# Unread full-array products in front of the scores, and a second weight pair fetched ahead, in a fused attention and gated-MLP kernel

## The chip, the cores and the metric

The kernel runs on one core of one Trainium2 chip. The core has a matrix engine (TensorE, here PE, with PEld for the loads of its stationary operand), a vector engine (VectorE, DVE), a scalar engine for activations (ScalarE, ACT), a general engine (GpSimd, POOL) and a queue from which most transfers are issued (SyncE, SP). The time is device microseconds for one execution; the number that counts is the median of several runs. One further execution was profiled.

## The reference

One transformer block with 2048 rows of 640 features, 32 heads of 20 features each, and a gated MLP of width 1728. Only these lines matter:

```
h  = x + attention(layernorm(x), wqkv, wo)      # softmax(q k^T / sqrt(20)) v, 32 heads
h2 = h + ((ln(h) @ w_gate) * (ln(h) @ w_up)) @ w_down
```

Inputs and weights are bf16; the output is h2.

## The kernel before

**Score steps.** The 32 heads are eight groups of four. A head takes 32 partitions of a 128-partition tile, so the scores of four heads are four products that each use 32 rows of the array (L497). Their keys are a 128-column slice of `kT` and their queries 512 (or 256) columns of `qa` or `qb`. Products are collected until a score tile `sc` of 1536 columns, three PSUM banks, is full. There are two such tiles, and one step of the main loop fills one. In all there are 683 steps. ACT then takes the exponential of the tile into `E` (L510). In some steps the last 512 columns go to DVE instead, which computes the exponential by a polynomial in four instructions (L538, L547, L548, L543); ACT then handles 1024 columns. The values product takes `E` as its moving operand and `vx` as its stationary one, with 32 output columns for each head (L690), and collects in `acc`.

**Order.** The Python code is a planner. It runs through the steps one by one and writes down every engine's instructions in a fixed order; nothing is reordered on the chip. It keeps its own clocks in `at`: `at["pe"]` for PE, `at["dve"]` for DVE, `at["exp"]` for the end of the last exponential, and `at["slot"]` for the times at which the score tiles come free. In each step it calls `emit_S` (scores and exponential), `emit_AV` (values products), events that are due, and then `run_job`, which fills PE up to a moment a little ahead of ACT's next need. After that `spare` gives DVE what is left of its time. `x_takes` decides whether DVE takes a third of a tile; one of its conditions is that DVE's clock is not far ahead of PE's.

**Jobs.** The rest of the block is cut into generators. `job_proj` and `job_V` make q, k and v (L292, L306). `job_out` multiplies by `wo` (L926), adds x, and makes the second layer norm and its transposes (L272). `job_glu` computes gate and up products (L999 when 512 rows are handled at once, L1017 in `glu_pair` for 256), and `job_y` multiplies by `w_down` (L1058) and stores. Each `yield` tells the planner how long the piece takes on PE. Most of these products use all 128 rows and 128 columns of the array; transposes and products with the identity do too.

**Keep-warm products.** After step 58, where no job ran and there is room by the planner's clocks, `keep_warm` issues two products of the identity with 512 columns of `kT[0]` into a `mi` bank that nothing reads (L467). There are 69 such pairs.

**Weights of the gated MLP.** `w_up` and `w_gate` come in seven pairs of tiles, `fp` 0 to 6, each tile 320 KB (L972, issued from SP). They sit in a pool with two buffers for each name, `wu` and `wg`, so two pairs fit at a time. `job_glu` is run for the first query block whole, then for halves of 256 rows: its keys are (0,0), (1,0), (2,0), (2,2), (3,0). It asks for a pair when the pair before it starts. When it starts its last pair it fetches pair 0 for the next job (`late["next"]`). In the later jobs pairs 3 to 6 are resident, in the tiles of the queries that are no longer needed (`load_res`, once the last query block begins), and only pairs 0 to 2 are streamed. After the last score step `last_tail` finishes the last half block.

Of the kernel before, what the change touches and what calls it, by code (L numbers as in the profile page):

```python
# [36 lines left out]
BANK = 512  # L37
# [17 lines left out]
WARM, LEAD = 58, 3  # L55
# [4 lines left out]
RES_STEPS = 3  # L60
WO_NS, SUMS_NS, ROOT_NS, ROWS_NS = 1500, 6000, 5000, 5000
END_OF_TIME = 10 ** 9
X_LEAST, X_OUT, X_SOON = 3, 6, 4
E_BUFS = 6
SHIFT = 544.0
# [13 lines left out]
def kernel(  # L79
# [11 lines left out]
    nc = tc.nc  # L91
# [22 lines left out]
    ident = const.tile([P, P], BF16, name="ident")  # L114
# [15 lines left out]
    kT = [qkp.tile([P, S], BF16, name=f"kT{g}") for g in range(NG)]  # L130
# [12 lines left out]
    at = {"pe": 0, "dve": 0, "mi": 0, "acc": 0, "slot": [0, 0], "exp": 0, "av": {}}  # L143
# [140 lines left out]
    def q_of(g, b, c0, w):  # L284
        return qb[g][:, c0:c0 + w] if b == NB - 1 else qa[g][:, b * QB + c0:b * QB + c0 + w]
# [47 lines left out]
    for s, (p, g, lo, hi, _) in enumerate(segs):  # L333
        w = PASS[p][2]
# [28 lines left out]
    cur = {"key": None, "gen": None, "fresh": True}  # L363
# [23 lines left out]
    def first():  # L387
        return urgent and (opens.get(urgent[0][0], 0) < at["pe"] + SWITCH or not (waiting or jobs or cur["gen"]))

    def step():  # L390
        if cur["fresh"] and (first() or waiting):
            if cur["gen"] is not None:
                jobs.appendleft((cur["key"], cur["gen"]))
            cur["key"], cur["gen"] = (urgent if first() else waiting).popleft()
        c = advance()
        if c == WAIT:
            waiting.append((cur["key"], cur["gen"]))
            cur["gen"] = None
            c = advance() if jobs and not any(w[0][1:] == jobs[0][0][1:] for w in waiting) else NEXT
        if c is None:  # L400
            return None
        if c == FREE:
            advance()
            return FREE
        if cur["fresh"] and c not in (END, NEXT):
            at["pe"] = max(at["pe"], at["mi"] if cur["key"] != ON_ACC else 0) + SWITCH
        cur["fresh"] = c in (END, NEXT)
        if cur["fresh"]:
            if cur["key"] != ON_ACC:
                at["mi"] = max(at["mi"], at["dve"] + LAT)  # L410
        else:
            at["pe"] += c
        return c

    def advance():
        if cur["gen"] is None:
            if not jobs:
                return None
            cur["key"], cur["gen"] = jobs.popleft()
        try:  # L420
            return next(cur["gen"])
        except StopIteration:
            done.add(cur["key"])
            cur["gen"] = None
            return END

    def ensure(key):
        while key not in done:
            if step() is None:
                raise RuntimeError(f"no job for {key}")  # L430
# [30 lines left out]

    COST = {"T": 300, "v": 680, "nf": 780}

    def keep_warm():
        ps = bank()
        for _ in range(2):
            nc.tensor.matmul(ps[:], lhsT=ident[:], rhs=kT[0][:, 0:BANK], start=True, stop=True)  # L467
# [19 lines left out]
    def emit_S(i):  # L487
        sc = scp.tile([P, EW], F32, name="sc")
        us, n = tiles[i]
        for s, kt, j, _ in us:  # L490
            p, g = segs[s][0:2]
            ensure(("k", g, kt // TPB))
            ensure(("q", PASS[p][0], g))
        for s, kt, j, o in us:
            p, g = segs[s][0:2]
            b, c0, w = PASS[p]
            nc.tensor.matmul(  # L497
                sc[:, o:o + w],
                lhsT=kT[g][SLOT * j:SLOT * (j + 1), kt * P:(kt + 1) * P],
                rhs=q_of(g, b, c0, w)[SLOT * j:SLOT * (j + 1), :],  # L500
                start=True, stop=True)
        begin = max(at["pe"], at["slot"][-2])
        at["pe"] = begin + S_NS
        start = max(at["exp"], begin + S_EXP)
        n_act, took = n, None
        if start == at["exp"] and x_takes(i):
            n_act = n - BANK
            took = emit_x(sc[:, n_act:n], [(s, kt, j, o - n_act) for s, kt, j, o in us if o >= n_act])
        e = ep.tile([P, EW], BF16, name="E")
        exps = nc.scalar.activation(e[:, 0:n_act], sc[:, 0:n_act], ACT.Exp, bias=EXP_BIAS, scale=SM_SCALE)  # L510
        if took is not None:
            tc.declare_no_dep(exps.ins, took.ins, reason="both only read the score tile, in different banks")
        run = EXP_NS + n_act * EXP_COL
        free = start + run + EXP_END
        at["slot"].append(free if took is None else max(free, at["dve"] + LAT))
        at["exp"] = start + run
        for s, kt, j, o in us:
            if o < n_act:
                av_q.append((i, s, kt, j, e[:, o:o + PASS[segs[s][0]][2]]))
# [4 lines left out]
    def x_takes(i):  # L524
        us, n = tiles[i]
        s = us[-1][0]
        return (n == EW and segs[s][4] == "only" and (PASS[segs[s][0]][0] < LAST_B or X_LAST(segs[s][0])) and last_tile[s] - i >= X_LEAST and len({u[0] for u in us}) == 1
                and len(x_open) < 2 and at["dve"] < at["pe"] + TOL and len(x_live) < X_OUT)

    def emit_x(ps, us):  # L530
        s = us[0][0]
        w = PASS[segs[s][0]][2]
        v = xp.tile([P, BANK], F32, name="xv", bufs=2)
        u = v[:].bitcast(U16).rearrange("p (n h) -> p n h", h=2)[:, :, 0]
        t = xp.tile([P, BANK], F32, name="xt", bufs=2)
        e = xp.tile([P, BANK], I16, name="xe", bufs=X_OUT)
        dve(690)
        took = nc.vector.tensor_scalar(v[:], ps, X_SCALE, X_BASE, ALU.mult, ALU.max)  # L538
        x_live.append((s, us[-1][1], us[-1][2]))
        x_left[s] = x_left.get(s, 0) + 1  # L540

        def last():
            nc.vector.scalar_tensor_tensor(e[:], t[:], X_R, v[:], ALU.mult, ALU.add)  # L543
            x_left[s] -= 1
            x_put.append([(now["i"], s, kt, j, e[:, o:o + w].bitcast(BF16)) for s, kt, j, o in us])
        x_open.append((s, deque([
            lambda: nc.vector.scalar_tensor_tensor(t[:], u, X_P, u, ALU.add, ALU.mult),  # L547
            lambda: nc.vector.scalar_tensor_tensor(t[:], t[:], X_Q, u, ALU.add, ALU.mult),  # L548
            last])))
        x_last[0] = x_open[-1]  # L550
        return took
# [233 lines left out]
    def gen_ln(ch):  # L785
        ts = range(ch * TPB, (ch + 1) * TPB)
        mv = small.tile([P, TPB, 2], F32, name="mv")
        while at["pe"] < x_at.get(ch, END_OF_TIME) and not now["forced"]:
            yield WAIT
# [96 lines left out]
        nc.sync.dma_start(qsp[g][:, QA:S], qb[g][:])  # L886


    late = {"res": {}}

    def open_late():
        rx.release()
# [80 lines left out]
        return view  # L973

    def load_w(fp, st):
        if fp == 0 and "next" in late:
            st["w", fp] = late.pop("next")
        elif fp in st["res"]:
            st["w", fp] = st["res"][fp]
        else:  # L980
            st["w", fp] = [w_tile(src, fp, late["w"].tile([P, KT * FPW], BF16, name=nm))
                           for nm, src in (("wu", B_w_up), ("wg", B_w_gate))]
# [28 lines left out]
    def glu_pair(st, fp, f2, c0, n):  # L1011
# [13 lines left out]
                yield 216 * n // QB  # L1025
        yield NEXT

    def job_glu(st, ts, order=tuple(range(FP)), more=False):
        c0, n = ts[0] * P, len(ts) * P
        hold = {}  # L1030
        if "hh" not in st:
            st["hh"] = [late["h"].tile([P, QB], BF16, name=f"hh{f}") for f in range(2 * FP)]
        for k, fp in enumerate(order):
            for nx in order[k:k + 2]:
                if ("w", nx) not in st:
                    load_w(nx, st)
            if more and k == FP - 1:
                ahead = {"res": {}}
                load_w(0, ahead)
                late["next"] = ahead["w", 0]  # L1040
            for f2 in range(2):
                if n <= HW and end["pool"] is None:
                    yield from glu_pair(st, fp, f2, c0, n)
                    continue
                for m in range(2):
                    yield from glu_sum(st, fp, f2, m, c0, n, hold)
        for fp in range(FP):
            del st["w", fp]

    def job_y(st, ts, store_halves=False):  # L1050
        for t in ts:
# [184 lines left out]
    i = 0  # L1236
# [134 lines left out]
```

## Time and profile before

| what | value |
|---|---|
| median of 3 runs | 942.64 us (939.83 to 942.7) |
| the profiled execution | 945.22 us, of which the span is 943.4 us |
| mean granted PE clock over the span | 0.984 |
| first to last exponential of a score tile | 15.4 to 899.3 us |
| PE, waiting for a score tile to be freed by ACT | 43.6 us in 103 waits |

How the rows of the profile are read: a group has the line, the engine, the operation, output<-inputs by name, the shapes, the count, then the busy time and the mean duration in ns, then the idle time of the engine directly before these instructions and what ended it. In a row of windows the columns are the stretch, its length, the busy time and number of instructions of PE, PEld, DVE, ACT and POOL, the clock that PE was granted (1.00 is full), the share of the DMA engines and GB/s. In a row of the timeline the first two numbers are start and duration in us, and the bracket gives the idle time before it and its releaser. Matmuls are pipelined, so that the durations of neighbours overlap, and exponentials overlap their neighbours by some 0.1 to 0.4 us.

### The profile page before, as it was taken

Reading aid. Unit: us, or ns where it says so; the run is one execution under the profiler, and the core shown is the slowest. Engines: PE = TensorE matmul, PEld = TensorE weight load, DVE = VectorE, ACT = ScalarE, POOL = GpSimd, SP = SyncE. Lnnn points to the kernel's source line nnn. Section 1 sums busy time; section 2 is a strip of 40 time slices with the busy share of each in tenths; the row PEclk is TensorE's granted clock in tenths of the full one; section 3 lists DMA queues with packets and bytes.
Section 4 is the critical chain, followed back from the end, with each engine's and each line's share of the span. In section 5 each row is a group of like instructions: output and inputs, shape, how many; then the busy total and the mean of one; then the engine's idle time right before and its main releaser. Section 6 shows DMA issues by size and latency. Waiting matters only on the chain.

```text
span 943.4 us, 20070 instructions
## 1 busy us (share of the span) xinstructions
PE 832.4 (88%) x8087; PEld 348.2 (37%) x8087; DVE 668.8 (71%) x1333; ACT 882.6 (94%) x719; POOL 62.2 (7%) x160
## 2 busy tenths in 40 slices
PE   8788898889988899988898998998898889978897
PEld 5233232222232222332233333444433444434565
DVE  7673358898888888888887667777688667372342
ACT  6999999999999999999999999999899999998941
POOL 4210011000000000000000000000000000000000
PEclk9999999999999999999999999899899999998999
DMA  6000010011150122115100322011601301002310
GB/s 189 28 2 1 1 31 21 13 35 27 41 163 13 29 69 61 48 55 198 27 13 21 85 69 63 3 42 53 179 6 41 87 10 48 15 8 69 77 43 17
DMA packets 75515, 47.20 MB, mean 50 GB/s; under 512 B 20412, under 2 KB 71752, under 8 KB 75416
## 3 DMA queue, kind: packets, MB, share of 16 engines
q1 hardware_dynamic: 75416, 45.86, 17.8%
q8 instruction: 65, 1.06, 0.5%
q14 instruction: 34, 0.28, 0.1%
HBM read 38.53 MB, written 7.30 MB: 49 GB/s over the span
## 4 chain that ended last, share of the span: by engine, by line
ACT 44%; PE 31%; issue 15%; DVE 8%; DMA 1%; SPq 0%; ACTq 0%
ACT E L510 44%; PE sc L497 7%; PE acc L690 5%; PE mi L1058 4%; PE mi L999 3%; PE mi L1017 3%; PE mi L292 2%; PE f L999 2%; PE f L1058 2%; PE mi L306 1%; DMA wg<-in_B_w_gate_dram 1%; DVE xt L548 1%; PE mi L926 1%; DVE st L194 1%; PE mi L467 1%
## 5 line engine op out<-in xcount | busy, mean ns | idle before, releaser
L510 ACT ACTIVATE E<-sc 128x1536 bf16<-128x1536 f32 (+1 forms) x683 | 865.1, 1434 | 19.5 <-PE sc L497 16.1
L497 PE MATMUL sc<-qa,kT 32*128 32x512 bf16 (+1 forms) x1920 | 203.3, 341 | 41.7 <-ACT E L510 32.8
L497 PEld LDWEIGHTS <-kT 32*128 32x128 bf16 x2816 | 85.9, 92 | 261.2 <-issue 215.2
L690 PE MATMUL acc<-E,vx 128*32 128x256 bf16 (+1 forms) x2624 | 172.8, 329 | 0.6 <-ACT E L510 0.6
L538 DVE TENSOR_SCALAR xv<-sc 128x512 f32<-128x512 f32 x144 | 98.8, 688 | 47.1 <-PE sc L497 45.3
L548 DVE SCALAR_TENSOR_TENSOR xt<-xt,xv 128x512 f32<-128x512 f32 x144 | 102.5, 719 | 0.8
L543 DVE SCALAR_TENSOR_TENSOR xe<-xt,xv 128x512 int16<-128x512 f32 x144 | 102.2, 714 | 0.9
L547 DVE SCALAR_TENSOR_TENSOR xt<-xv 128x512 f32<-128x512 uint16 x144 | 101.3, 717 | 0.3
L292 PE MATMUL mi<-lnT,wp 128*128 128x512 bf16 x305 | 83.8, 381 | 8.9 <-DVE kT L299 3.8
L613 POOL TENSOR_TENSOR on<-asb,bc 128x256 bf16<-128x256 f32 (+1 forms) x35 | 37.1, 1059 | 698.3 <-DMA bc<-scr 433.8
L690 PEld LDWEIGHTS <-vx 128*32 128x32 bf16 x2816 | 56.5, 96 | 67.3 <-issue 66.6
L497 PE MATMUL sc<-qb,kT 32*128 32x256 bf16 (+1 forms) x896 | 69.7, 293 | 11.6 <-ACT E L510 10.8
L1058 PE MATMUL mi<-wd,hh 128*128 128x320 bf16 x350 | 63.3, 302 | 2.2 <-DVE xr L1062 2.2
L1058 PEld LDWEIGHTS <-hh 128*128 128x128 bf16 x448 | 38.0, 97 | 39.6 <-issue 28.5
L1022 DVE CAST u<-mi 128x256 bf16<-128x256 f32 (+1 forms) x42 | 17.7, 422 | 40.3 <-PE mi L1017 39.9
L292 PEld LDWEIGHTS <-wp 128*128 128x128 bf16 x310 | 25.1, 97 | 53.0 <-issue 39.1
L690 PE MATMUL acc<-xe,vx 128*32 128x512 bf16 (+1 forms) x192 | 44.5, 330 | 0.0
L467 PE MATMUL mi<-kT,ident 128*128 128x512 bf16 x138 | 41.7, 384 | 2.1 <-DVE hh L1024 0.6
L926 PE MATMUL mi<-wo,on 128*128 128x320 bf16 x224 | 40.9, 309 | 2.2 <-DVE xr L930 2.1
L999 PE MATMUL mi<-ln2T,wu 128*128 128x512 bf16 (+1 forms) x140 | 39.1, 389 | 3.9 <-DVE hh L1007 3.9
L999 PE MATMUL mi<-ln2T,wg 128*128 128x512 bf16 (+1 forms) x140 | 38.7, 382 | 3.4 <-DVE u L259 3.4
L299 DVE TENSOR_SCALAR kT<-mi,one_row 128x512 bf16<-128x512 f32 x30 | 22.4, 745 | 26.8 <-PE mi L292 26.5
(150 smaller groups left out, 630.3 us busy)
## 6 DMA issues: line engine op xcount, KB each, us to landing
wu<-in_B_w_up_dram SPq DMA_DIRECT2D x24, 320.0 KB
wg<-in_B_w_gate_dram SPq DMA_DIRECT2D x24, 320.0 KB
bc<-scr SPq DMA_DIRECT2D x80, 64.0 KB
qsp<-qa SPq DMA_DIRECT2D x8, 384.0 KB
xr<-in_A_x_dram SPq DMA_DIRECT2D x16, 160.0 KB
bc<-scr SPq DMA_DIRECT2D x76, 32.0 KB
out_dram<-xr SPq DMA_DIRECT2D x14, 160.0 KB
wd<-in_B_w_down_dram SPq DMA_DIRECT2D x13, 160.0 KB
```

The source lines that it names most:

```text
L292: nc.tensor.matmul(ps[:], lhsT=wslice(m, g, c), rhs=lnT[:, c, ch * QB:(ch + 1) * QB], start=(c == 0), stop=(c == KT - 1))
L467: nc.tensor.matmul(ps[:], lhsT=ident[:], rhs=kT[0][:, 0:BANK], start=True, stop=True)
L497: nc.tensor.matmul(sc[:, o:o + w], lhsT=kT[g][SLOT * j:SLOT * (j + 1), kt * P:(kt + 1) * P], rhs=q_of(g, b, c0, w)[SLOT * j:SLOT * (j + 1) ...
L510: exps = nc.scalar.activation(e[:, 0:n_act], sc[:, 0:n_act], ACT.Exp, bias=EXP_BIAS, scale=SM_SCALE)
L538: took = nc.vector.tensor_scalar(v[:], ps, X_SCALE, X_BASE, ALU.mult, ALU.max)
L543: nc.vector.scalar_tensor_tensor(e[:], t[:], X_R, v[:], ALU.mult, ALU.add)
L547: lambda: nc.vector.scalar_tensor_tensor(t[:], u, X_P, u, ALU.add, ALU.mult),
L548: lambda: nc.vector.scalar_tensor_tensor(t[:], t[:], X_Q, u, ALU.add, ALU.mult),
L690: nc.tensor.matmul(acc["t"][SLOT * j:SLOT * (j + 1), 0:w], lhsT=vx[kt][:, VS * h:VS * h + SLOT], rhs=e, start=(acc["n"][j] == 0), stop=(ac ...
L926: nc.tensor.matmul(ps[:, 0:HALF], lhsT=on[g][:, t * P:(t + 1) * P], rhs=wo[g][:, cs], start=(g == 0), stop=(g == NG - 1))
L999: nc.tensor.matmul(ps[0:M, 0:n], lhsT=st["w", fp][k][:, c, f2 * P:f2 * P + M], rhs=st["ln2T"][:, c, c0:c0 + n], start=(c == 0), stop=(c == ...
L1058: nc.tensor.matmul(ps[:, 0:HALF], lhsT=st["hh"][f][0:K, t * P:(t + 1) * P], rhs=late["Wd"][f][0:K, cs], start=(f == 0), stop=(f == 2 * FP ...
```

## The change

There are two edits. The planner now keeps a list, `full`, of what it has put on PE with the full array: every piece of a job (apart from the short piece of a normalisation job) and the keep-warm pairs. `cool()` asks whether less than 520 ns of it lies in the last 2400 ns by the planner's clock. If so, `emit_S` issues one product of the identity with 512 columns of `kT[0]` into the first bank of the score tile, just before the scores that overwrite it, and adds 216 ns to PE's clock. Nothing reads that product. The second edit fetches pair 1 of the next GLU job, as well as pair 0: it is asked for when a GLU job has ended.

```diff
+FULL_IN, FULL_NS = 2400, 520
...
         else:
             at["pe"] += c
+            if cur["key"][0] != "nf" or c > 780 or c == 515:
+                full.append((at["pe"], c))
         return c
...
+    full = deque()
+
+    def cool():
+        now_ = max(at["pe"], at["slot"][-2])
+        while full and full[0][0] < now_ - FULL_IN:
+            full.popleft()
+        return sum(f[1] for f in full) < FULL_NS
+
     def keep_warm():
+        full.append((at["pe"], 430))
         ps = bank()
...
             ensure(("q", PASS[p][0], g))
+        if i > WARM and cool():
+            at["pe"] = max(at["pe"], at["slot"][-2]) + 216
+            full.append((at["pe"], 216))
+            nc.tensor.matmul(sc[:, 0:BANK], lhsT=ident[:], rhs=kT[0][:, 0:BANK], start=True, stop=True)
         for s, kt, j, o in us:
...
-        if fp == 0 and "next" in late:
-            st["w", fp] = late.pop("next")
+        if fp in late["next"]:
+            st["w", fp] = late["next"].pop(fp)
...
+    def load_next(fp):
+        ahead = {"res": {}}
+        load_w(fp, ahead)
+        late["next"][fp] = ahead["w", fp]
+
     def job_glu(st, ts, order=tuple(range(FP)), more=False):
...
             if more and k == FP - 1:
-                ahead = {"res": {}}
-                load_w(0, ahead)
-                late["next"] = ahead["w", 0]
+                load_next(0)
...
         for fp in range(FP):
             del st["w", fp]
+        if more:
+            load_next(1)
```

More of the change, by code (lines that the diff above doesn't have):

```diff
@@ L886, in spill @@
         nc.sync.dma_start(qsp[g][:, QA:S], qb[g][:])
-    late = {"res": {}}
+    late = {"res": {}, "next": {}}
     def open_late():
```

## The prediction

> **What bounds the kernel now.** I read the page first, then ACT's waits from 60 us on, then windows of 3.41 us around each fall of the PE clock, then ACT's exponentials place by place.
>
> ```profile
> span 943.4 us, 20070 instructions
> ...
> PE 832.4 (88%) x8087; PEld 348.2 (37%) x8087; DVE 668.8 (71%) x1333; ACT 882.6 (94%) x719; POOL 62.2 (7%) x160
> ```
>
> ```profile
> ACT E L510 <- PE sc L497: 14.1, 20, 3.2
> ```
>
> ACT is busy for 94% of the span and its exponentials (E from sc, L510) set the pace of the loop. What can be won inside the loop is the time in which ACT waits for scores: 14.1 us after the first 60 us, in 20 waits. The next table shows where the clock is (columns: stretch, its length, busy time and instructions of PE, PEld, DVE, ACT, POOL, then the granted clock, DMA share, GB/s).
>
> ```profile
> 308.92:312.33 3.41, 3.41 (x19) 0.65 (x16) 2.83 (x5) 2.64 (x3) 0.00 (x0) 0.50 0.02 5
> 585.39:588.81 3.42, 2.77 (x45) 1.42 (x40) 3.19 (x9) 3.25 (x4) 1.02 (x1) 1.00 0.06 19
> 588.81:595.63 6.82, 5.92 (x57) 2.69 (x57) 4.78 (x9) 5.59 (x5) 0.00 (x0) 0.50 0.01 2
> ...
> 660.49:663.90 3.41, 3.38 (x22) 1.08 (x21) 0.84 (x3) 1.33 (x2) 0.00 (x0) 0.50 0.23 40
> ...
> 677.55:680.97 3.42, 3.42 (x17) 1.19 (x20) 2.94 (x5) 2.45 (x3) 0.00 (x0) 0.50 1.08 318
> ...
> 715.10:718.52 3.42, 3.42 (x21) 1.11 (x19) 3.18 (x4) 2.48 (x3) 1.43 (x1) 0.50 0.49 138
> ...
> 855.05:861.87 6.82, 6.56 (x52) 2.58 (x51) 1.27 (x3) 4.21 (x3) 0.00 (x0) 0.50 0.38 98
> 810.68:814.09 3.41, 2.62 (x38) 1.37 (x31) 0.63 (x2) 3.41 (x4) 0.73 (x1) 1.00 0.12 39
> 814.09:817.50 3.41, 3.08 (x52) 1.72 (x55) 0.79 (x3) 3.41 (x4) 0.00 (x0) 1.00 0.01 2
> ```
>
> The clock halves for whole stretches of 3.41 us, eight of them inside the loop (two of the rows hold two). ACT, nearly always busy, loses time in each. PE was not idle before: 2.77 of 3.42 us busy in 585.39:588.81. What those earlier stretches lack is products over all 128 rows and 128 columns. PE's groups in 585.39:588.81, in 711.69:715.10, in 851.64:855.05, and, where the clock held, in 810.68:814.09:
>
> ```profile
> L999 PE MATMUL mi<-ln2T,wu 128*64 128x512 bf16 x1 | 0.4, 404 | 0.0
> ...
> L272 PE MATMUL mi<-ident,ln 128*128 128x128 bf16 x7 | 0.7, 221 | 0.0
> ...
> L1017 PE MATMUL mi<-ln2T,wu 128*128 128x256 bf16 x3 | 0.6, 297 | 2.2 <-DMA wu<-in_B_w_up_dram 2.2
> ...
> L467 PE MATMUL mi<-kT,ident 128*128 128x512 bf16 x2 | 0.6, 386 | 0.0
> ```
>
> Up to 7 x 128 = 896 full-array columns in a stretch, the next ran at half clock; with 2 x 512 = 1024 it did not. The scores (32 rows) and the value products (32 columns) fill the rest and do not hold it. What ACT lost, one group row for each place (308.92:313.5, 588.81:597, 660.49:666, 677.55:681, 715.1:719.7, 745:751, 853:863):
>
> ```profile
> L510 ACT ACTIVATE E<-sc 128x1024 bf16<-128x1024 f32 (+1 forms) x4 | 5.2, 1404 | 1.3 <-PE sc L497 1.3
> ...
> L510 ACT ACTIVATE E<-sc 128x1536 bf16<-128x1536 f32 (+1 forms) x6 | 8.1, 1383 | 1.8 <-PE sc L497 1.8
> ...
> L510 ACT ACTIVATE E<-sc 128x1536 bf16<-128x1536 f32 x4 | 5.7, 1451 | 2.4 <-PE sc L497 2.4
> ...
> L510 ACT ACTIVATE E<-sc 128x1536 bf16<-128x1536 f32 (+1 forms) x3 | 3.8, 1306 | 1.0 <-PE sc L497 1.0
> ...
> L510 ACT ACTIVATE E<-sc 128x1536 bf16<-128x1536 f32 (+1 forms) x3 | 3.9, 1338 | 0.9 <-PE sc L497 0.9
> ...
> L510 ACT ACTIVATE E<-sc 128x1536 bf16<-128x1536 f32 x5 | 7.1, 1461 | 1.3 <-PE sc L497 1.3
> ...
> L510 ACT ACTIVATE E<-sc 128x1536 bf16<-128x1536 f32 x5 | 7.1, 1449 | 4.1 <-PE sc L497 4.1
> ```
>
> They add up to 12.8 of the 14.1 us. The first, second, fourth and fifth, 5.0 us over five cold stretches, are the clock alone: 1.0 us for each. The third, sixth and seventh, 7.8 us, begin with a wait for weights:
>
> ```profile
> 850.74 0.42 SPq L972 DMA_DIRECT2D wu<-in_B_w_up_dram  x1
> 851.22 1.72 SPq L972 DMA_DIRECT2D wg<-in_B_w_gate_dram  x1
> 853.03 0.47 SPq L972 DMA_DIRECT2D wu<-in_B_w_up_dram  x1
> ...
> 854.74 0.99 PE L1017 MATMUL mi<-ln2T,wu 128*128 128x256 bf16 x5 [2.18 <-DMA wu<-in_B_w_up_dram]
> 855.99 0.34 PEld L1017 LDWEIGHTS <-wg 128*128 128x128 bf16 x3 [0.74 <-DMA wg<-in_B_w_gate_dram]
> ```
>
> These are the loads of pair 1 of a GLU job: asked for when the job starts, landed 4.0 us (wu) and 4.8 us (wg) after issue, later than pair 0 is used up. PE then stands before the scores of the next step, and the gap also empties the stretch that decides the clock.
>
> **The change part by part.** I compared the built programs' instruction order. The new one has 54 unread products (512 columns, in front of the scores of 54 of the 683 steps), 14 fewer of the old keep-warm products (138 to 124), six more thirds of a score tile taken from ACT by DVE (144 to 150), four pair-1 loads earlier, and one streamed pair fewer because a later job finds it resident. From about step 645 on, and in all of the tail, the order of PE is the same, so the gain or loss must arise in the loop.
>
> *The early loads.* Pair 1 is asked for at the end of the GLU job before; the outputs of one half of a query block and the projections of the next stand between. All three waits go, with the cold stretches they start: -7.8 us. Eight DMA issues move ahead of small ones (sums, scr, the output) on SP; their rows above take 0.42 to 1.72 us on the queue, and what is queued behind them feeds normalisations several steps later, so I charge nothing; uncovered, they would cost a few us once. Next late would be pair 2, asked for when pair 0 is used up. The halves of pair 1 show the room it has:
>
> ```profile
> 748.58 0.72 PE L1017 MATMUL mi<-ln2T,wu 128*128 128x256 bf16 x5 [0.54 <-DMA wu<-in_B_w_up_dram]
> ...
> 751.81 0.71 PE L1017 MATMUL mi<-ln2T,wu 128*128 128x256 bf16 x5 [0.64 <-DVE hh L1024]
> ```
>
> A half takes 3.2 us, a pair 6.5 us, against 4.0 to 4.8 us of landing: it holds, by about 2 us.
>
> *The clock.* -5.0 us if all five other cold stretches go. I counted, in each order, the steps from 60 on in which three neighbouring steps hold fewer than two 512-column full-array products (transposes by their columns, 64-column products half): 17 before, 4 after. The 8 cold stretches times 4/17 leave 1.9, at 1.0 us each: +1.9 us.
>
> *The 54 products.* Their price from rows of their kind:
>
> ```profile
> 540.92 1.24 PE mi L999 x5
> ```
>
> ```profile
> L467 PEld LDWEIGHTS <-ident x138: 94/97/100, 122.1 to 891.1; 128*128 128x128 bf16 x138
> L467 PE MATMUL mi<-kT,ident x138: 375/380/391, 122.4 to 891.3; 128*128 128x512 bf16 x138
> ```
>
> Five products in 1.24 us, the last lasting 0.38, follow each other at (1.24 - 0.38)/4 = 0.215 us; with a bare weight load 0.097 us more: 0.31 us each. No chain in the trace has such a product in front of scores. Upper bound: each delays ACT fully, 54 x 0.31 = 16.7 us. Lower bound: 0, since nothing reads them and a gain is already counted in the clock. What hides them is PE's own wait for the score buffer, and the time from scores to their exponential:
>
> ```profile
> 811.33 6.88 ACT L510 ACTIVATE E<-sc 128x1536 bf16<-128x1536 f32 x5
> ...
> 814.24 0.40 PE L497 MATMUL sc<-qb,kT 32*128 32x256 bf16 x6 [0.40 <-ACT E L510]
> ```
>
> ```profile
> L510 ACT ACTIVATE E<-sc 128x1536 bf16<-128x1536 f32 x538 | 747.3, 1525 | 16.7 <-PE sc L497 14.5 <-ACT E L510 0.2
> L510 ACT ACTIVATE E<-sc 128x1024 bf16<-128x1024 f32 x145 | 153.8, 1097 | 2.8 <-PE sc L497 1.5 <-ACT E L510 0.3
> ```
>
> Five exponentials in 6.88 us are one per (6.88 - 1.52)/4 = 1.34 us. The one that starts at 811.33 + 3 x 1.34 = 815.35 reads scores done by 814.64: 0.7 us of room, more than 0.31. The product waits with the scores for the same buffer, so what queues behind it on PE is those scores, then the value products and the job. Where a job has run over, the room is less. Outside the seven places ACT lost 14.1 - 12.8 = 1.3 us in a handful of waits of about 0.2 us; I take seven more of these, +1.5 us, near the lower bound because the row just shown is the nearest.
>
> *DVE's six more pieces.* Each shortens an exponential by 1525 - 1097 = 428 ns: -2.6 us. It adds four DVE instructions of about 0.7 us, 17 us in all:
>
> ```profile
> L543 DVE SCALAR_TENSOR_TENSOR xe<-xt,xv 128x512 int16<-128x512 f32 x144 | 102.2, 714 | 0.9
> ```
>
> DVE is busy for 71%, so they are covered; uncovered, evacuations would come late (a rival).
>
> Sum against the profiled execution (945.2 us: span 943.4 and 1.8 around it): -7.8 - 5.0 + 1.9 + 1.5 - 2.6 = -12.0, so 933.2. The median shown, 942.64, lies 2.6 below that execution, whose eight cold stretches may be more than usual; since what is left does not hang on them, I do not scale, and predict 933.
>
> **The rivals.**
>
> *The clock still falls (0.16).* The early loads work, but idling, not the lack of full-array columns, decides the clock. Then the sum is without -5.0 + 1.9: -7.8 + 1.5 - 2.6, 936.3, or 938 with a cold stretch or two left near the loads. For it: 711.69:715.10 and 851.64:855.05 also hold long PE waits. Against it: 585.39:588.81, 81% busy. The Trainium skill, "TensorE: Matmul & The Clock Gate", section on HAM oscillation, asks only that PE have no idle gap over about 3.4 us; by that rule none of the five would have gone cold and the products change nothing. The trace does not agree (2.77 of 3.42 us busy, then 0.50).
>
> *Pair 2 is late instead (0.10).* Its issue cannot come before pair 0 is used up. If SP's queue holds it as it held pair 1, about half of 7.8 us comes back: 937.
>
> *DVE binds (0.08).* Six pieces hold evacuations in crowded steps; 17 us at 0.2 exposed: 936.6.
>
> *The products delay the scores (0.08, the other side).* Price 0.31 us in front of scores on PE, place steps 109 to 677, and it decides when the room after the scores is under 0.31 us in most of the 54 steps, as it is when a job ran just before. Then +16.7 instead of +1.5: 948.4, slower. Against it: 0.7 us of room at 814 us, and a product is placed when recent jobs were few.
>
> **How the numbers follow.** Forecast 0.58 (own range 930 to 936). 0.3% is about what a measurement can tell from no change: 939.8 to 945.5 around the median. Faster: the forecast, most of the first three rivals (0.13 + 0.09 + 0.06), 0.86. Same: what is left of those three, 0.06. Slower: 0.08. The range goes from 929 (no cost, no cold stretch left: 929.8) to 939.5, past the milder rivals; the slow one and the tails are left out.
>
> **What would show it.** After: no wait of PE for wu or wg in the three GLU jobs; cold stretches in the loop down from eight to three or fewer; ACT's wait for scores from 14.1 to about 4 us; L510 with 532 long and 151 short forms; the span after the last exponential unchanged. Wrong if cold stretches remain although two full-array products stood before them, if ACT's waits begin behind the new products, or if waits for pair 2 appear.

## The result, and the profile after

| | before | changed |
|---|---|---|
| median of 4 runs each, same chip | 942.0 us (939.83 to 942.7) | 933.2 us (930.96 to 934.68) |
| ratio | | 0.9908, 95% interval [0.9882, 0.9935] |
| the profiled execution, its span | 945.22 us, 943.4 us | 934.68 us, 932.5 us |
| end of the last exponential of a score tile | 899.3 us | 888.5 us |
| cold stretches of 3.41 us after step 58 and before that end | 8 | 2 |

The time fell by 8.8 us; 933 us had been forecast. The page of the changed kernel (its scores are L513, its exponentials L526, its values products L706, its gate and up products for 256 rows L1033, the new unread products L509; the kernels of the experiments differ from it by a line or two):

```profile
span 932.5 us, 20108 instructions
...
PE 827.1 (89%) x8059; PEld 349.0 (37%) x8127; DVE 682.0 (73%) x1357; ACT 880.0 (94%) x719; POOL 62.3 (7%) x160
```

ACT has the same share as before of a shorter span, and DVE is busy for 13 us more. The exponentials by shape, and ACT's waits from 60 us on (total, times, longest), in the changed kernel:

```profile
L526 ACT ACTIVATE E<-sc 128x1536 bf16<-128x1536 f32 x532 | 735.6, 1494 | 9.2 <-PE sc L513 7.5
L526 ACT ACTIVATE E<-sc 128x1024 bf16<-128x1024 f32 x151 | 156.5, 1070 | 1.2 <-PE sc L513 0.6
```

```profile
ACT E L526 <- PE sc L513: 4.7, 15, 1.0
```

The wait for scores is down from 14.1 to 4.7 us, and there are the 532 long and 151 short exponentials. The GLU job of the third half block on PE's timeline (pair 1 is the one that starts at 850.32):

```profile
850.32 0.72 PE L1033 MATMUL mi<-ln2T,wu 128*128 128x256 bf16 x5
850.88 0.49 PE L1033 MATMUL mi<-ln2T,wg 128*128 128x256 bf16 x3
...
853.01 0.72 PE L1033 MATMUL mi<-ln2T,wu 128*128 128x256 bf16 x5
```

No bracket follows these rows: PE did not wait for wu or wg in this job, nor in that of the first half block. In the job of the second half block a wait is left, now for pair 2. PE's last products of pair 0, then the transfers on SP and the loads of pair 2 into the array:

```profile
745.38 0.71 PE L1033 MATMUL mi<-ln2T,wg 128*128 128x256 bf16 x5
...
747.15 0.32 SPq L620 DMA_DIRECT2D scr<-ri  x1
748.96 1.71 SPq L623 DMA_DIRECT2D bc<-scr  x4
750.72 0.42 SPq L988 DMA_DIRECT2D wu<-in_B_w_up_dram  x1
...
753.88 0.67 PEld L1033 LDWEIGHTS <-wu 128*128 128x128 bf16 x5 [0.68 <-DMA wu<-in_B_w_up_dram]
754.94 0.33 PEld L1033 LDWEIGHTS <-wg 128*128 128x128 bf16 x4 [0.40 <-DMA wg<-in_B_w_gate_dram]
```

Pair 0 was used up at 746.1 us, but the issue of pair 2 stands on SP behind `scr` and four `bc` and came 4.6 us later. The exponential behind this wait came 0.4 us late. In a second profile of the same kernel (e6 below) PE waited longer at this place:

```profile
PE mi L1033 <- DMA wu<-in_B_w_up_dram: 1.3, 1, 1.3
PE mi L1033 <- DMA wg<-in_B_w_gate_dram: 0.3, 1, 0.3
```

There the exponential came 1.3 us late, and the only two cold stretches of that profile after step 58 (752.68 to 759.50 us) follow directly. A wait for pair 2 is one of the things that the prediction named as proof against it.

The one place after step 58 where the clock still fell in the first profile, in windows (columns as in the prediction), and PE's groups in the stretch before the fall, 588.34 to 591.76:

```profile
588.34:591.76 3.42, 2.42 (x25) 0.97 (x19) 3.15 (x9) 3.26 (x4) 0.41 (x1) 1.00 0.02 5
591.76:595.17 3.41, 3.41 (x33) 1.57 (x33) 1.70 (x3) 2.93 (x3) 0.00 (x0) 0.50 0.00 0
595.17:598.58 3.41, 3.41 (x32) 1.22 (x30) 2.42 (x5) 1.94 (x2) 0.00 (x0) 0.50 0.00 0
```

```profile
L513 PE MATMUL sc<-qa,kT 32*128 32x256 bf16 x18 | 1.2, 273 | 0.0
L509 PE MATMUL sc<-kT,ident 128*128 128x512 bf16 x3 | 1.1, 379 | 1.0 <-ACT E L526 1.0
L637 PE MATMUL mi<-identf,asb 128*128 128x4 f32 x4 | 0.6, 258 | 0.0
```

Here stand three of the new products, two of them wholly inside (they start at 588.57 and 590.18), and the clock fell all the same. This too the prediction named as proof against it. The stretch has no value product at all, which the last section comes back to.

### The profile page after: what moved, and what is told of

Same layout as the page of the kernel before. It is cut to its first block, busy times and chain, and to the rows that moved or that the text cites. A ratio compares the mean times of both kernels' runs of the same rounds, so it can differ in the third digit from the quotient of the medians.

```text
span 932.5 us, 20108 instructions
## 1 busy us (share of the span) xinstructions
PE 827.1 (89%) x8059; PEld 349.0 (37%) x8127; DVE 682.0 (73%) x1357; ACT 880.0 (94%) x719; POOL 62.3 (7%) x160
## 4 chain that ended last, share of the span: by engine, by line
ACT 46%; PE 29%; issue 16%; DVE 7%; DMA 1%; ACTq 0%
ACT E L526 46%; PE sc L513 7%; PE acc L706 5%; PE mi L1079 4%; PE mi L293 2%; PE mi L1015 2%; PE f L1015 2%; PE f L1079 2%; PE mi L307 1%; PE mi L1033 1%; PE mi L942 1%; DVE st L195 1%; PE sc L509 1%; DVE xe L559 1%; DVE xt L563 1%
## 5 line engine op out<-in xcount | busy, mean ns | idle before, releaser
L526 ACT ACTIVATE E<-sc 128x1536 bf16<-128x1536 f32 (+1 forms) x683 | 862.6, 1400 | 10.4 <-PE sc L513 8.1
L513 PE MATMUL sc<-qa,kT 32*128 32x512 bf16 (+1 forms) x1920 | 202.7, 341 | 32.1 <-ACT E L526 21.4
L513 PEld LDWEIGHTS <-kT 32*128 32x128 bf16 x2816 | 83.6, 91 | 249.0 <-issue 210.4
L706 PE MATMUL acc<-E,vx 128*32 128x256 bf16 (+1 forms) x2612 | 170.0, 328 | 0.6 <-ACT E L526 0.6
L554 DVE TENSOR_SCALAR xv<-sc 128x512 f32<-128x512 f32 x150 | 102.7, 687 | 35.6 <-PE sc L513 34.1
L559 DVE SCALAR_TENSOR_TENSOR xe<-xt,xv 128x512 int16<-128x512 f32 x150 | 105.2, 708 | 1.0
L564 DVE SCALAR_TENSOR_TENSOR xt<-xt,xv 128x512 f32<-128x512 f32 x150 | 105.0, 710 | 0.8
L563 DVE SCALAR_TENSOR_TENSOR xt<-xv 128x512 f32<-128x512 uint16 x150 | 103.6, 706 | 0.4
L706 PEld LDWEIGHTS <-vx 128*32 128x32 bf16 x2816 | 56.1, 96 | 66.0 <-issue 65.4
L513 PE MATMUL sc<-qb,kT 32*128 32x256 bf16 (+1 forms) x896 | 68.2, 288 | 7.0 <-ACT E L526 5.3
L706 PE MATMUL acc<-xe,vx 128*32 128x256 bf16 (+1 forms) x204 | 43.8, 327 | 0.0
L1015 PE MATMUL mi<-ln2T,wg 128*128 128x512 bf16 (+1 forms) x127 | 36.1, 382 | 4.3 <-DVE u L260 3.5
L1033 PE MATMUL mi<-ln2T,qa 128*128 128x256 bf16 (+1 forms) x240 | 34.2, 274 | 4.7 <-DVE hh L1040 4.0
```

What stands on the lines that cost most here:

```text
L513: nc.tensor.matmul(sc[:, o:o + w], lhsT=kT[g][SLOT * j:SLOT * (j + 1), kt * P:(kt + 1) * P], rhs=q_of(g, b, c0, w)[SLOT * j:SLOT * (j + 1) ...
L706: nc.tensor.matmul(acc["t"][SLOT * j:SLOT * (j + 1), 0:w], lhsT=vx[kt][:, VS * h:VS * h + SLOT], rhs=e, start=(acc["n"][j] == 0), stop=(ac ...
L1015: nc.tensor.matmul(ps[0:M, 0:n], lhsT=st["w", fp][k][:, c, f2 * P:f2 * P + M], rhs=st["ln2T"][:, c, c0:c0 + n], start=(c == 0), stop=(c == ...
L1033: nc.tensor.matmul(ps[0:M, k * n:(k + 1) * n], lhsT=st["w", fp][k][:, c, f2 * P:f2 * P + M], rhs=st["ln2T"][:, c, c0:c0 + n], start=(c == ...
```

## The experiments

Each kernel ran beside the kernel before. The result of each run gives its time and its mean granted clock, and the two go together: over the 139 runs of the twelve experiments and of the kernel before beside them, a fit with one level for each kernel and one common slope gives 6.6 us for 0.01 of mean clock (95%: 6.2 to 7.0), and leaves a scatter of 0.8 us. A cold stretch lowers the mean clock by 3.41 x 0.5 / 933 = 0.0018, which is 1.2 us. The fit lets each time be split into its clock and the rest: the last column is the level at a clock of 0.99 with its 95% bounds. e3 and e7 are one kernel and share theirs. The level of the kernel before differs by up to 0.7 us between the three chips, so that smaller differences between kernels of different chips say nothing.

| kernel | products | accounting | early loads | thirds | median us | ratio, 95% interval | mean clock | us at 0.99 |
|---|---|---|---|---|---|---|---|---|
| before (53 runs, 3 chips) | 0 | no | no | 144 | 943.7; 943.4; 944.0 | | 0.9859 | 941.3 ± 0.3 |
| e1_products_only | 54 | yes | no | 150 | 938.06 | 0.992 [0.9891, 0.9949] | 0.9913 | 938.8 ± 0.5 |
| e2_loads_only | 0 | no | yes | 144 | 937.84 | 0.9922 [0.9893, 0.9951] | 0.9896 | 937.2 ± 0.5 |
| e3_no_product_same_plan | 0 | yes | yes | 150 | 932.41 | 0.9867 [0.9813, 0.992] | 0.9864 | 929.8 ± 0.5 |
| e7_no_product_again | 0 | yes | yes | 150 | 932.35 | 0.9876 [0.9847, 0.9905] | (with e3) | (with e3) |
| e11_plan_only | 0 | yes | no | 150 | 932.31 | 0.9888 [0.9862, 0.9913] | 0.9873 | 930.5 ± 0.6 |
| e6_changed_again | 54 | yes | yes | 150 | 934.34 | 0.9887 [0.9862, 0.9913] | 0.9948 | 936.5 ± 0.7 |
| e4_two_products | 108 | yes | yes | 150 | 938.86 | 0.9932 [0.9907, 0.9957] | 0.9981 | 944.0 ± 0.6 |
| e5_narrow_product | 54 narrow | yes | yes | 150 | 931.43 | 0.9871 [0.9846, 0.9896] | 0.9954 | 935.2 ± 0.7 |
| e8_products_by_area | 20 | yes | yes | 150 | 933.4 | 0.9878 [0.9848, 0.9908] | 0.9893 | 932.3 ± 0.6 |
| e9_loads_more_thirds | 0 | no | yes | 153 | 930.43 | 0.9865 [0.9839, 0.9891] | 0.9900 | 930.5 ± 0.6 |
| e10_plan_fewer_thirds | 0 | yes | yes | 142 | 939.59 | 0.9961 [0.9937, 0.9986] | 0.9911 | 939.9 ± 0.4 |
| e12_double_accounting | 0 | doubled | yes | 146 | 931.17 | 0.9871 [0.9843, 0.9899] | 0.9882 | 929.5 ± 0.6 |

"Accounting" means the list `full`, the test `cool()` and the 216 ns that it adds to the planned clock of PE. They change the plan (which step runs how much of a job, which tiles give a third to DVE) also where no product is issued.

A second count comes from the traces. An exponential of 1536 columns ends 1.343 us after the one before it when nothing holds it up, and one of 1024 columns 0.917 us after. What goes beyond that is called its delay here. An exponential counts as one of a cold stretch if it starts in it or within 1.5 us of its end.

### The parts alone

**Without the early loads.**

```diff
-        if more:
-            load_next(1)
```

> The products with the old loads (pair 1 is again asked for when its GLU job starts). Theory: two separate gains. The clock part stays, so cold stretches in the loop after step 58 are at most about four, but the waits of PE for wu and wg come back in the jobs of 256 rows and cost ACT some 4 to 7 us: 937 to 940 us. Rival (the products alone carry the gain, the loads were covered by them): within 1 us of the changed kernel, 933 us, with no exponential kept waiting by wu or wg.

938.06 us: 5.6 better than before and 4 to 5 worse than the whole change. PE's waits for weights are as long as before (3.6 us in all, 3.3 there), one for pair 1 of the third half block and one for pair 2 of the second:

```profile
PE mi L1033 <- DMA wu<-in_B_w_up_dram: 2.9, 2, 2.0
PE mi L1033 <- DMA wg<-in_B_w_gate_dram: 0.7, 2, 0.4
```

Beside the products the loads are worth 938.8 - 936.5 = 2.3 us at equal clock, and 0.0035 of clock, another 2.3 us.

**The early loads alone**, with the order of before on PE.

```diff
-        if i > WARM and cool():
+        if False:
```

> The early loads of pair 1 without any product in front of scores; PE's order is that of the kernel before. Theory: the waits for wu and wg go, the cold stretches that come from too few full-array products stay (five to eight in the loop): 935 to 938 us. Rival (the cold stretches all come from the waits for weights): they go with the waits, 933 us or less.

937.84 us. ACT's wait for scores, and the fall that stays where before had one, preceded by a stretch with full clock:

```profile
ACT E L526 <- PE sc L513: 7.6, 17, 1.0
```

```profile
586.61:590.02 3.41, 1.94 (x23) 0.97 (x23) 3.38 (x9) 3.25 (x4) 1.03 (x1) 1.00 0.00 1
590.02:596.85 6.83, 6.76 (x59) 3.00 (x58) 3.96 (x7) 5.18 (x5) 0.00 (x0) 0.50 0.01 2
```

The wait is nearly halved, PE waits for no weights, and six cold stretches are left of eight. In the plan of before the loads are worth 4.1 us at equal clock and 0.0037 of clock (2.4 us).

**All but the product itself.** The accounting stays, so that every other instruction is where the changed kernel has it.

```diff
         if i > WARM and cool():
             at["pe"] = max(at["pe"], at["slot"][-2]) + 216
             full.append((at["pe"], 216))
-            nc.tensor.matmul(sc[:, 0:BANK], lhsT=ident[:], rhs=kT[0][:, 0:BANK], start=True, stop=True)
```

> The changed kernel with its 54 unread products left out and everything else the same, the planner's 216 ns for each included, so that the order of all other instructions and DVE's 150 thirds are as in the changed kernel. Theory: it is the products' effect on the clock that counts; five or more cold stretches in the loop after step 58, 4 to 6 us over the changed kernel: 937 to 939 us. Rival (the gain comes from the shifted plan and DVE's six more thirds, and the products only cost PE time): equal to the changed kernel or up to 2 us faster, 931 to 933 us.

932.41 us: nothing is lost without the products. The pair was run again on one chip.

> The changed kernel beside the next two on one chip. Theory: 0.990 to 0.991 of the kernel before. Rival: the run without products was only a faster chip or luck with the grid of the clock, and this one comes out equal to it.

> The run without products and with the same plan, again. Theory: the products cost about what they win, so it lies within 2 us of the changed kernel, on either side. Rival (the products decide): 4 us or more slower than the changed kernel.

934.34 us with the products and 932.35 without; the intervals of the ratios overlap, so that the products are worth nothing that these runs can tell, or cost a little. The clock is another matter: 0.9948 with them, 0.9864 without, and 5 and 7 cold stretches in the two profiles without against 2 and 2 with them. The products do keep the clock up, by 0.0084 or 5.6 us, and at equal clock they cost 936.5 - 929.8 = 6.7 ± 0.9 us.

**The accounting alone**, without early loads and without products.

```diff
-            nc.tensor.matmul(sc[:, 0:BANK], lhsT=ident[:], rhs=kT[0][:, 0:BANK], start=True, stop=True)
...
-        if more:
-            load_next(1)
```

> The accounting alone, with neither early loads nor products: 150 thirds, 62 keep-warm pairs. If plan and loads add up: 943.5 less the 5.4 us by which the accounting bettered the early loads alone, 938, ratio 0.994, with waits of PE for wu and wg of pair 1 as before. If the plan is worth something only where the loads are early: 941 to 943.

932.31 us. The parts do not add up: a plan that issues no product and loads nothing early gets the whole gain. PE still waits for the weights in it (the waits, and the place on PE's timeline):

```profile
PE mi L1032 <- DMA wu<-in_B_w_up_dram: 1.5, 2, 0.8
PE mi L1032 <- DMA wg<-in_B_w_gate_dram: 0.7, 2, 0.4
```

```profile
842.24 0.72 PE L1032 MATMUL mi<-ln2T,wu 128*128 128x256 bf16 x5 [0.62 <-DMA wu<-in_B_w_up_dram]
843.35 0.50 PE L1032 MATMUL mi<-ln2T,wg 128*128 128x256 bf16 x3 [0.39 <-DMA wg<-in_B_w_gate_dram]
```

The waits are 2.2 us in all, and the exponential behind the two on the timeline comes 1.1 us late, where that of before came 3.3 us late. The exponentials directly behind waits for weights are late by 6.6 us in all in the kernel before (three places, pair 1), by 3.4 in e1, by 2.0 here (pair 2 of the second half block, pair 1 of the third), by 0 in e2. With accounting and early loads pair 2 of the second half block is left: 1.5 and 1.8 us in e3 and e7, 0.4 and 1.3 in the two profiles of the changed kernel. So the plan and the loads take away in part the same waits, and together they can win these only once. Without and with the early loads this plan takes 930.5 and 929.8 us at equal clock: here they are worth 0.7 ± 0.8 us, not told apart from nothing.

### What a product costs

The changed kernel and e3 run the same steps, so that the delays of the exponentials that stand behind a product can be compared one by one. They are sorted by the exponential before (products within a cold stretch left out):

| | behind a 1024-column exponential | behind a 1536-column exponential |
|---|---|---|
| the same steps without product (e3) | 0.0 us | 0.0 us |
| changed, in two profiles | 1.9 and 2.0 us, 19 products | 0.0 us, 33 and 35 products |
| narrow product (e5) | 1.2 us, 19 | 0.2 us, 33 |
| two products (e4) | 6.0 us, 19 places | 0.4 us, 34 places |

A hidden one, on the timeline of the changed kernel around 402 us; the scores follow the product and the three exponentials run on without a gap:

```profile
401.69 3.71 ACT L526 ACTIVATE E<-sc 128x1024 bf16<-128x1024 f32 x3
402.76 0.38 PE L509 MATMUL sc<-kT,ident 128*128 128x512 bf16 x1 [0.52 <-ACT E L526]
403.07 0.39 PE L513 MATMUL sc<-qa,kT 32*128 32x512 bf16 x3
```

And two that are not hidden, behind two short exponentials in a row (the two end the group that starts at 502.80), first the changed kernel, then the same steps in e3:

```profile
502.80 3.57 ACT L526 ACTIVATE E<-sc 128x1536 bf16<-128x1536 f32 x3
...
504.52 0.38 PE L509 MATMUL sc<-kT,ident 128*128 128x512 bf16 x1 [0.39 <-ACT E L526]
504.83 0.40 PE L513 MATMUL sc<-qa,kT 32*128 32x256 bf16 x6
...
505.70 0.39 PE L509 MATMUL sc<-kT,ident 128*128 128x512 bf16 x1
506.02 0.40 PE L513 MATMUL sc<-qa,kT 32*128 32x256 bf16 x6
...
506.54 1.45 ACT L526 ACTIVATE E<-sc 128x1536 bf16<-128x1536 f32 x1 [0.17 <-PE sc L513]
```

```profile
498.65 6.19 ACT L525 ACTIVATE E<-sc 128x1536 bf16<-128x1536 f32 x5
...
500.37 0.40 PE L512 MATMUL sc<-qa,kT 32*128 32x256 bf16 x6 [0.40 <-ACT E L525]
...
501.29 0.40 PE L512 MATMUL sc<-qa,kT 32*128 32x256 bf16 x6
```

In e3 the scores start when the tile is free, and ACT runs through five exponentials. With products the scores start 0.3 us later; a tile behind a short exponential has 1.343 - 0.917 = 0.43 us less time, and ACT stands still for 0.17 us.

So the delays directly behind the products are 1.9 us. All delays outside cold stretches are 15.3 and 15.4 us in the two profiles of the changed kernel, 11.7 and 10.3 without products. The first and third of these hold the delay behind the wait for pair 2 (0.4 and 1.5 us); the other two have it in a cold stretch. Without it the products bring 4.6 to 5.2 us more: 1.9 directly, about as much again in the next four steps (1.8 us in the changed kernel against e3, 2.0 in e6 against e7), and some 1 us further on. That value products and jobs come later on PE there is the likely reason, not a shown one. The rest up to 6.7 us isn't placed.

**Two products at each place.**

```diff
-            nc.tensor.matmul(sc[:, 0:BANK], lhsT=ident[:], rhs=kT[0][:, 0:BANK], start=True, stop=True)
+            for _ in range(2):
+                nc.tensor.matmul(sc[:, 0:BANK], lhsT=ident[:], rhs=kT[0][:, 0:BANK], start=True, stop=True)
```

> Two unread products in place of one at each of the 54 places, the plan unchanged. Theory: a product costs ACT little because PE waits there for the score tile anyway; each more costs at most about the 1.5 us that the sum charged for the 54, and the remaining cold stretches become rarer: 932 to 935 us. Rival (the products delay the scores): 54 x 0.215 = 11.6 us more, 940 to 945 us.

938.86 us, between the theory's 932 to 935 and the rival's 940 to 945. The second product costs 944.0 - 936.5 = 7.5 us at equal clock, and wins 0.0033 of clock, 2.2 us. The runs of e4 lie at a clock of 0.996 to 0.999, so its level at 0.99 hangs on the common slope; but its delays outside cold stretches, 22.9 us against 15.4 in e6, are 7.5 us more too. ACT waits twice as often as in the changed kernel, and one fall is left:

```profile
ACT E L527 <- PE sc L514: 7.4, 29, 0.8
```

```profile
878.69:882.10 3.41, 2.79 (x43) 1.66 (x38) 1.52 (x5) 3.41 (x4) 0.00 (x0) 1.00 1.12 299
882.10:885.51 3.41, 3.41 (x20) 0.88 (x18) 0.42 (x1) 2.62 (x2) 0.00 (x0) 0.50 0.09 22
```

**A product of 32 output columns**, as long as the other but a quarter as wide.

```diff
-            nc.tensor.matmul(sc[:, 0:BANK], lhsT=ident[:], rhs=kT[0][:, 0:BANK], start=True, stop=True)
+            nc.tensor.matmul(sc[0:SLOT, 0:BANK], lhsT=ident[:, 0:SLOT], rhs=kT[0][:, 0:BANK], start=True, stop=True)
```

> The 54 unread products use 32 columns of the array in place of 128; the plan, the number of moving columns and PE's time for them are unchanged. Theory now, from the four runs so far: such a product costs what the full one costs (the changed kernel lost about 3.6 us more to waits at full clock than the run without products) but counts a quarter for the clock, so cold stretches come back as without products: four to six, 2 to 3 us over the changed kernel and over the run without products. Rival (PE's time counts for the clock, whatever part of the array works): as the changed kernel, three or fewer cold stretches.

Missed: it kept the clock as high (0.9954) as the full-array product. Windows of this kernel, and PE's groups in the first of them:

```profile
802.67:806.08 3.41, 2.91 (x44) 1.39 (x43) 1.00 (x4) 3.41 (x3) 0.67 (x1) 1.00 0.16 53
806.08:809.50 3.42, 3.34 (x50) 1.71 (x39) 0.42 (x1) 3.42 (x4) 0.00 (x0) 1.00 0.00 0
```

```profile
L513 PE MATMUL sc<-qb,kT 32*128 32x256 bf16 x18 | 1.2, 273 | 0.0
L509 PE MATMUL sc<-kT,ident 128*32 128x512 bf16 x2 | 0.8, 376 | 0.5 <-ACT E L526 0.4
L706 PE MATMUL acc<-E,vx 128*32 128x256 bf16 x16 | 0.6, 275 | 0.0
L637 PE MATMUL mi<-identf,asb 128*128 128x4 f32 x4 | 0.6, 258 | 0.0
L706 PE MATMUL acc<-xe,vx 128*32 128x256 bf16 x4 | 0.4, 278 | 0.0
```

Not one bf16 product of the full array stands in the stretch, and the next one ran at full clock. The rule of the prediction, that only the full array counts, does not hold. At equal clock the narrow products cost 935.2 - 929.8 = 5.4 us.

**Products only where the used area is small.** `area` collects jobs and keep-warm pairs in full and scores and value products at a quarter of their time; 20 of the 54 products remain.

```diff
+                area.append((at["pe"], c))
...
+        area.append((at["pe"], n * 5 / 48))
...
+        area.append((at["pe"], ready * w * 5 / 48))
...
+            if small_area():
+                area.append((at["pe"], 216))
                 nc.tensor.matmul(sc[:, 0:BANK], lhsT=ident[:], rhs=kT[0][:, 0:BANK], start=True, stop=True)
```

> The plan of the changed kernel, but the product is issued only where the array's working area is small: full-array work, plus a quarter of the scores' and the values products' columns, under 950 ns in the last 2400 by the planner's clocks. That leaves 20 of the 54. Theory (the clock goes by the working area, and each product costs some 0.07 us): cold stretches as rare as in the changed kernel or rarer, and two thirds of the products' price saved: 2 to 3 us faster than the changed kernel, 1 to 3 faster than without products. Rival (full-array columns alone decide): cold stretches as without products, no gain over that run.

933.4 us, no better than none. At equal clock the 20 cost 932.3 - 929.8 = 2.5 us, in proportion to the 54, and the clock rose from 0.9864 to 0.9893, in proportion too (0.0029 of 0.0084). Six cold stretches after step 58 are in its profile, against five and seven without products. So choosing the places by this count won nothing; whether the planner's clock or the count is at fault is not shown.

### What the plan wins

Two readings were set against each other: the thirds that DVE takes, and the reserve that the added 216 ns leave on PE. e9 is e2 with one line changed in `x_takes`:

```diff
-                and len(x_open) < 2 and at["dve"] < at["pe"] + TOL and len(x_live) < X_OUT)
+                and len(x_open) < 2 and at["dve"] < at["pe"] + TOL + 200 and len(x_live) < X_OUT)
```

> The early loads alone, without product or accounting, but DVE may be 400 ns ahead of PE by the planner's clocks instead of 200 when it takes a third of a score tile: 153 thirds (144 before, 150 with the change), 55 keep-warm pairs. Theory T (the thirds are what the changed plan wins): nine thirds at 428 ns are 3.9 us off the early loads' 937.8, so 934, a ratio near 0.990. Theory R (the 216 ns that the accounting adds to PE's planned clock act as a reserve, so that jobs end earlier and scores are less often late): 937 to 938, ratio 0.994, and ACT waits for scores stay at 7 us or more.

e10 is e3 with `TOL - 100` in that line:

> Early loads and accounting, no product, but DVE may be only 100 ns ahead of PE when it takes a third: 142 thirds and 65 keep-warm pairs instead of 150 and 62. T: eight thirds at 428 ns lost against 932.4, so 935.8, ratio 0.992. R: 932 to 933, ratio 0.988.

e12 is e3 with `+ 432` in place of `+ 216`:

> Early loads, no product, and 432 instead of 216 ns added to PE's planned clock at each place: 146 thirds, 56 keep-warm pairs. T: four thirds fewer than with 216, so 932.4 + 1.7 = 934, ratio 0.990. R: the doubled reserve takes still more of the small waits, 930 or less, ratio 0.986; beyond some point jobs fall behind and the time rises again.

Neither reading forecast the sizes: 930.43 us in e9 and 939.59 in e10 lie beyond both, on the side of the thirds, and 931.17 in e12 lies nearer to the reserve's forecast. Nine more thirds gave 937.2 - 930.5 = 6.7 us at equal clock, where 3.9 were to be had by their 428 ns each; eight fewer took 10.1, where 3.4 were. Double accounting with four thirds fewer changed nothing (929.5 against 929.8), where the thirds alone would have cost 1.7. ACT's waits for scores from 60 us on, of e9, e10 and e12, each from its own trace:

```profile
ACT E L526 <- PE sc L513: 5.1, 12, 1.0
```

```profile
ACT E L525 <- PE sc L512: 7.2, 15, 1.4
```

```profile
ACT E L525 <- PE sc L512: 3.6, 11, 0.7
```

Neither reading stands alone. The delays show where much of the difference lies, in the exponentials whose width is not that of the one before them, that is where a third begins or ends:

| | before | e2 | e10 | e9 | e12 | e3, e7, e11 |
|---|---|---|---|---|---|---|
| thirds | 144 | 144 | 142 | 153 | 146 | 150 |
| all delays outside cold stretches, us | 15.7 | 14.7 | 16.6 | 13.7 | 12.8 | 11.7, 10.3, 11.9 |
| of these, at a change of width, us | 7.0 | 7.1 | 7.3 | 6.3 | 4.5 | 3.5, 3.4, 3.4 |
| of these, directly behind a wait for weights, us | 1.1 | 0 | 0 | 0 | 0.7 | 1.5, 0, 2.0 |

The plan with 216 ns accounted wins 2.6 us by the six thirds and some 3.5 us where all of them begin and end, 6.1 of the 7.4 us by which it betters e2 at equal clock. e10 has the same accounting and lost these 3.5 us again, so that the reserve by itself does not bring them. What is left is in which steps the thirds fall, beside which jobs; that is argued and was not tested by itself. Why these steps suit and others don't stays open; the runs only show that a shift of 100 ns in the planner's test moves the time by 10 us at equal clock (7 in the medians).

No kernel here is shown to beat the changed one: e9 (930.43 us), e12, e5 and the plan without products have lower medians, but their intervals overlap with 0.9887 [0.9862, 0.9913].

## Why the prediction was right, and where not

The total, the sign and most of the signs to look for came out (8 cold stretches to 2, 14.1 to 4.7 us of waits, 532 and 151, and 44.0 us behind the last exponential, as before). The wait for wu and wg did not go in all three jobs, and all three signs of being wrong appeared in part: a fall behind two full-array products, waits of ACT behind the new products, and a wait for pair 2. The terms of the sum were less good than the sum.

*The early loads, -7.8 us.* The mechanism is right for pair 1: its waits are gone. The size depends on the rest: 6.5 us in the plan of before (4.1 and 2.4 by the clock), 4.6 beside the products, 0.7 at equal clock in the plan without them. Two steps failed. One took three waits seen in one plan as a price that every plan pays: in the changed plan without early loads (e11) exponentials came 2.0 us late behind weights instead of 6.6, so that part of these -7.8 us belongs to the plan. The other said of pair 2 that "it holds, by about 2 us", and gave its issue no delay on SP. In the order of before it held (e2 has no wait for weights); in the changed order it was issued 4.6 us after pair 0 was used up. So the rival that named pair 2 came true in part: ACT lost 0.4 us at that place in one profile and 1.3 in the other, there, with the two cold stretches behind it, 4 us between 746 and 764 us, half of the 7.8.

*The clock, -5.0 + 1.9 us.* The price of 1.0 us for a cold stretch was nearly right (1.2). The products do raise the clock, by 5.6 us against the same plan without them. The rule behind it, that "scores (32 rows) and the value products (32 columns) fill the rest and do not hold it", is wrong, as e5 and the stretch at 588.34 showed.

*The 54 products, +1.5 us.* Directly behind them the delays are 1.9 us, and the room after the scores does hide most of them, as the prediction said; the row it leaned on was one behind a long exponential, and there the cost is nil in every one of 33 cases. What failed is the end of that step: it priced each product at its own step. At equal clock they cost 6.7 us, of which 1.9 are directly behind them, some 3 in later steps and the rest not placed. So the products were not worth the 1.6 us net that -5.0 + 1.9 + 1.5 gives, but about nothing (+2.0 us between the two medians, not told apart from none).

*DVE's six more pieces, -2.6 us.* Mis-sized: as measured, this is the largest term. Together with the plan that they came with, they are worth 7.4 us at equal clock beside the early loads (937.2 to 929.8) and 10.8 without these (941.3 to 930.5). The prediction saw that the plan moved and counted its instructions, but not that the delays around all the thirds would fall.

Written again from the runs, in the order plan, loads, products, from the mean of before at its clock: -10.8 and -0.9 for the plan (level and clock), -0.7 and +0.6 for the loads, +6.7 and -5.6 for the products, together -10.7; in the order loads, plan, products: -4.1 - 2.4, -7.4 + 2.1, +6.7 - 5.6. The overestimates of loads and products and the underestimate of the plan cancelled; that the sum met the result within 0.2 us was luck. Of the other rivals, the one that the products would leave the clock as it was is refuted by the clock's 0.0084, and the one that they delay ACT fully by the 6.7 us that they cost instead of 16.7. Nothing shows DVE to bind: with three more pieces than the changed kernel gives it, in another plan, e9 was no slower.

## What to carry to other kernels

Where a planner writes the order of the instructions, an edit that adds a cost to its clock changes the whole plan: run the plan without the work, as e3 and e11 did, before a gain is put down to the work. When one wait for a buffer is taken away, look in the same job for the next one: here it was pair 2 behind small transfers on the same queue. Fill-in work in front of a critical product is free only where the stage it feeds has just begun a long piece; count the short ones. And when the clock varies from run to run, fit the time against it over all runs: that took the scatter here to 0.8 us, and showed two opposite effects of 6 us which the medians hid.

## What was not expected of the hardware

The clock followed the used part of the array better than anything else. In each stretch of 3.41 us at full clock, on the grid on which the falls lie, the streaming time of the products was added up: those of 128 rows and 128 columns in full, of 64 columns by half, scores (32 rows) and value products (32 columns) by a quarter, f32 products left out. A column was counted as 0.417 ns, about what the traces show (products of 512 columns follow each other at 0.215 us), and the streaming as begun 60 ns after the recorded start. Over the 13 profiles other than e5 there are 3198 such stretches between 26 and 885 us; the 42 that were followed by half clock all have 1.27 us or less, 37% of the stretch. Only 31 that kept the clock lie as low, and the ten lowest of these all hold 0.17 to 0.22 us of f32 products that the count leaves out. With the streaming begun 0 to 160 ns after the recorded start, the bound comes to 1.24 to 1.31 us, and 23 to 53 stretches that kept the clock lie below it. PE's busy time does not separate them: 2.42 of 3.42 us at 588.34 and, in e4, 2.79 of 3.41 at 878.69 were followed by a fall, 2.62 of 3.41 at 810.68 in the kernel before were not. The section on HAM oscillation of the Trainium skill's "TensorE: Matmul & The Clock Gate", which asks for no idle gap over about 3.4 us, does not cover these falls. In e5 two falls lie at 0.69 and 1.26 us and six stretches below that bound kept the clock, five of them at 0.83 to 1.08 us, three of these with no more than 0.01 us of f32 products: a narrow product may count for more than a quarter, which wasn't measured by itself. All of this was counted after the runs, and e8, which placed products by a like count on the planner's clock, kept its falls: it is what these traces show, not a rule that a run has tested.
